# k^T v in four 64x64 tiles of the array instead of two of 96 rows, with a second bank and a sum

## The chip, the cores and the metric

The kernel runs on one core of a Trainium2 chip. The metric is the device time of one execution in microseconds (us); lower is better.

## The reference

An attention without softmax is followed by a SwiGLU feed-forward, all in fp32:

```python
q, k, v: (8, 8, 576, 64)          # batch, heads, sequence, head size
kv  = einsum('bhsd,bhse->bhde', k, v)       # k^T v: 64 x 64 for each head, summed over 576 rows
out = einsum('bhsd,bhde->bhse', q, kv)
out = out / sqrt(mean(out * out, -1) + 1e-6) * g_norm
x   = out.transpose(0, 2, 1, 3).reshape(4608, 512)
result = (silu(x @ w_gate) * (x @ w_val)) @ w_out      # 512 -> 1536 -> 512
```

The change touches only the first `einsum`: 8 batches x 8 heads, each a contraction over 576 rows into 64x64.

## The kernel before

The 4608 tokens are worked off in nine blocks of 512. `Att(n)` is the attention of block n. k^T v of one batch is needed for each of blocks 0 to 7. Block 0 is done at once, because nothing else can run before it; the attention of block n+1 is woven into the feed-forward of block n. The parts that the change and the argument touch:

```python
KP = 96
KT = S // KP                      # 576 = 96 x 6: six chunks of 96 rows
a_psum = pool("a_psum", 1, space=PS)        # one bank a buffer
b_psum = pool("b_psum", 2, space=PS)
c_psum = pool("c_psum", 2, space=PS)
m_psum = pool("m_psum", 3, space=PS)

# class Att
def load(self, room=None):
    self.load_q()
    # ...
    for j in range(NS):                             # 4 head pairs
        hs = slice(2 * j, 2 * j + 2)
        for i, (tiles, src) in enumerate(((self.k, k), (self.v, v))):
            if room:                                # block 0: a tile named h lends its room
                t = room.rearrange("p f t -> p (f t)")[:, (2 * j + i) * 2 * KT * D :]
            else:
                t = ld_pool.tile([P, 2 * BLK], F32, name="ld")
            t = t[0:KP, 0 : 2 * KT * D].rearrange("p (h x) -> p h x", h=2)
            nc.sync.dma_start(out=t, in_=src[self.n, hs].rearrange("h (p t) d -> p h (t d)", t=KT))
            tiles.append(t.rearrange("p h (t d) -> p h t d", t=KT))

def kv(self, js):
    # ...
    if js[0] == 0:
        self.kv_ps = m_psum.tile([P, NS, D], F32, name="m")
    for j in js:
        for c in range(KT):
            for u in range(2):                      # two heads: two column positions
                nc.tensor.matmul(
                    self.kv_ps[u * D : (u + 1) * D, j, :], lhsT=self.k[j][:, u, c, :],
                    rhs=self.v[j][:, u, c, :], start=(c == 0), stop=(c == KT - 1),
                )
    if js[-1] == NS - 1:
        nc.scalar.copy(out=kvs[self.n % 3], in_=self.kv_ps)

def turn_q(self, i):                                # q into [d, token], through m_psum
    # ...
def product(self, i, pools=None):                   # q . kv: 64x64 in four positions, two banks
    # ...
    for u in range(2):
        sq = sq_pool.tile([P, 2, NS, D], F32, name="sq")
        nc.scalar.activation(out=sq, in_=self.ps[i][u], func=ACT.Square)
        nc.vector.tensor_reduce(out=self.z[:, i, u], in_=sq, axis=mybir.AxisListType.X, op=OP.add)

# program order
blocks[0].load(room)              # q, k, v of block 0: DMA issues on SyncE
weights(1)                        # five weight loads, also on SyncE; one weight rounded on VectorE/ScalarE
scaled = blocks[0].all()          # turn_q, kv, product, root, scale, turn_x
# ... block 0: plain_up (12 x), then plain_down(0), kv and turn_q of block 1,
#     plain_down(1..3) with block 1's product and the rest between
# ... blocks 1 to 8: loads of the next block, up(), down(), with two kv calls of two head pairs each
```

All DMA loads are issued by SyncE, in program order. `weights` also gives work to VectorE (four operations for each weight piece, named g, u, u and wg in the trace) and to ScalarE. Each engine has one list of instructions, whose order a scheduler fixes when the program is built.

## Time and profile before

| before | value |
|---|---|
| time, median of 6 runs | 1116.32 us (1115.74 to 1117.8) |
| span of the profiled run | 1113.7 us |
| TensorE busy | 98% of the span |
| k^T v: instructions in blocks 1 to 7, and in block 0 | 672 and 96 |
| start to first feed-forward matmul | 33.58 us |
| a k^T v call of two head pairs, block 2 | 1.55 us |

A timeline has a row for each group: start us, length us, engine, line, operation, out<-in, count, and in brackets the idle time before it and what ended it; "SPq" rows are DMA issues on SyncE.

Block 1: k^T v, the turn of q and the output matmuls of block 0 (L559) share TensorE. From the timeline of TensorE before, 127 to 136 us:

```profile
127.17 1.62 PE L237 MATMUL m<-ld 96*64 96x64 f32 x48
128.72 1.09 PE L251 MATMUL m<-ident,ld 128*128 128x128 f32 x8
...
131.52 0.92 PE L237 MATMUL m<-ld 96*64 96x64 f32 x24 [0.53 <-DMA ld<-in_v_dram]
...
134.79 0.92 PE L237 MATMUL m<-ld 96*64 96x64 f32 x24
```

Two head pairs come in one piece, then one, then one, with the turn of q between them.

### The profile page before, as it was taken

The page shows a single profiled execution, that of the slowest core. Times are in us where ns is not written, and L with a number is a line of the kernel's source. Part 1 is how long each engine was busy: PE and PEld are TensorE (multiplying, and loading weights), DVE is VectorE, ACT ScalarE, POOL GpSimd, SP SyncE. Part 2 cuts the span into 40 slices and gives each one's busy share as a digit, 9 for nine tenths or more (in the row PEclk, how much of TensorE's full clock was granted, in tenths as well). Part 3 has the DMA queues.
Part 4 walks back from the last instruction along what each step waited for, and adds up shares of the span by engine and source line. Part 5 has one row for each costly group of instructions (what it writes and reads, how often), then busy time and mean ns, then how long its engine had stood idle before and what let it go on. Part 6 is the DMA issues. An engine that isn't in the chain of part 4 may idle for free.

```text
span 1113.7 us, 15512 instructions
## 1 busy us (share of the span) xinstructions
PE 1092.4 (98%) x6528; PEld 901.2 (81%) x6528; DVE 444.2 (40%) x759; ACT 272.4 (24%) x460; POOL 401.0 (36%) x320
## 2 busy tenths in 40 slices
PE   5999999999999999999999999999999999999998
PEld 4444548888888888888888888888888888888887
DVE  2999333126322551156113721263124621561221
ACT  2655112222122212222222122221222122222210
POOL 0021003452344334442444334532543345424550
PEclk9999999999999999999999999999999999999999
DMA  9677410310122010300040012101200100000001
GB/s 273 194 221 186 109 54 19 86 39 1 39 51 51 23 38 26 77 23 26 13 102 23 1 39 61 42 22 38 52 19 1 38 1 1 1 30 10 1 1 38
DMA packets 70245, 57.62 MB, mean 52 GB/s; under 512 B 39456, under 2 KB 64032, under 8 KB 70176
## 3 DMA queue, kind: packets, MB, share of 16 engines
q1 hardware_dynamic: 70112, 56.63, 18.9%
q8 instruction: 51, 0.84, 0.3%
q14 instruction: 18, 0.15, 0.0%
q0 software_dynamic: 64, 0.00, 0.0%
HBM read 47.19 MB, written 9.44 MB: 51 GB/s over the span
## 4 chain that ended last, share of the span: by engine, by line
PE 89%; DVE 1%; DMA 0%; issue 0%
PE b L383 45%; PE c L383 22%; PE a L383 11%; PE b L559 4%; PE m L237 2%; PE m L271 2%; PE m L315 1%; PE m L251 1%; PE b L546 0%; PE c L546 0%; DVE u L150 0%; DMA ld<-in_v_dram 0%; DVE wo L154 0%; DVE g L149 0%; PE a L271 0%; DVE u L144 0%
## 5 line engine op out<-in xcount | busy, mean ns | idle before, releaser
L110 POOL TENSOR_TENSOR t<-wg,wv 128x512 f32<-128x512 f32 x96 | 123.9, 1292 | 182.5 <-PE b L383 92.0
L110 POOL TENSOR_TENSOR t<-wv 128x512 f32<-128x512 f32 x48 | 63.9, 1331 | 323.9 <-PE c L383 117.8
L109 DVE TENSOR_TENSOR s<-h 128x256 f32<-128x256 f32 x48 | 20.4, 425 | 307.8 <-POOL h L111 307.8
L110 POOL TENSOR_TENSOR t<-wo 128x512 f32<-128x512 f32 x72 | 91.4, 1269 | 121.5 <-PE c L383 70.6
L383 PE MATMUL b<-x,t 128*128 128x256 f32 x384 | 91.3, 381 | 0.8
L383 PE MATMUL b<-x,wg 128*128 128x256 f32 x384 | 92.0, 382 | 0.0
L109 DVE TENSOR_TENSOR u<-c,u 128x512 f32<-128x512 f32 x96 | 65.9, 687 | 63.1 <-ACT u L425 63.1
L383 PE MATMUL a<-x,wg 128*128 128x256 f32 x384 | 90.9, 379 | 0.0
L383 PE MATMUL c<-xs,t 128*128 128x256 f32 x384 | 90.8, 379 | 0.0
L383 PE MATMUL b<-xs,t 128*128 128x256 f32 x384 | 90.8, 379 | 0.0
L383 PE MATMUL c<-xs,wv 128*128 128x256 f32 x384 | 90.7, 379 | 0.0
L383 PE MATMUL b<-x,wv 128*128 128x256 f32 x384 | 90.7, 379 | 0.0
L383 PE MATMUL b<-t,h 128*128 128x256 f32 x384 | 86.3, 381 | 0.0
L383 PE MATMUL b<-wo,h 128*128 128x256 f32 x384 | 85.8, 379 | 0.0
L398 ACT COPY u<-b 128x512 f32<-128x512 f32 x56 | 32.8, 586 | 214.2 <-PE b L383 214.2
L383 PEld LDWEIGHTS b<-x,t 128*128 128x128 f32 x384 | 72.3, 190 | 12.0 <-issue 2.5
L383 PEld LDWEIGHTS c<-xs,t 128*128 128x128 f32 x384 | 72.9, 190 | 10.3 <-issue 0.4
L383 PEld LDWEIGHTS b<-xs,t 128*128 128x128 f32 x384 | 72.9, 190 | 10.1 <-issue 0.3
L383 PEld LDWEIGHTS b<-x,wv 128*128 128x128 f32 x384 | 73.0, 190 | 9.9
L383 PEld LDWEIGHTS c<-xs,wv 128*128 128x128 f32 x384 | 73.0, 190 | 9.9
L383 PEld LDWEIGHTS a<-x,wg 128*128 128x128 f32 x384 | 73.0, 190 | 9.9
L111 POOL TENSOR_TENSOR h<-s,u 128x512 f32<-128x512 f32 x48 | 60.9, 1269 | 54.7 <-DVE u L109 54.7
(88 smaller groups left out, 1534.5 us busy)
## 6 DMA issues: line engine op xcount, KB each, us to landing
out_dram<-o SPq DMA_DIRECT2D x18, 512.0 KB, 2.8
ld<-in_q_dram SPq DMA_DIRECT2D x32, 256.0 KB, 5.0
ld<-in_k_dram SPq DMA_DIRECT2D x28, 288.0 KB, 4.6
ld<-in_v_dram SPq DMA_DIRECT2D x28, 288.0 KB, 4.1
ld<-in_moe_w_gate_dram SPq DMA_DIRECT2D x12, 512.0 KB, 4.8
ld<-in_moe_w_val_dram SPq DMA_DIRECT2D x12, 512.0 KB, 5.2
ld<-in_moe_w_out_dram SPq DMA_DIRECT2D x12, 512.0 KB, 4.1
h<-in_k_dram SPq DMA_DIRECT2D x4, 288.0 KB, 6.2
```

The source lines that it names most:

```text
L109: add = lambda e, o, a, b: e.tensor_tensor(out=o, in0=a, in1=b, op=OP.add)
L110: sub = lambda e, o, a, b: e.tensor_tensor(out=o, in0=a, in1=b, op=OP.subtract)
L111: mul = lambda e, o, a, b: e.tensor_tensor(out=o, in0=a, in1=b, op=OP.mult)
L237: nc.tensor.matmul(self.kv_ps[u * D : (u + 1) * D, j, :], lhsT=self.k[j][:, u, c, :], rhs=self.v[j][:, u, c, :], start=(c == 0), stop=(c = ...
L251: nc.tensor.transpose(ps[:, j], self.q[t][:, j], ident)
L271: nc.tensor.matmul(self.ps[i][u][p : p + D, t, j, :], lhsT=self.qt[rows, 2 * i + t, j, p : p + D], rhs=kvs[b % 3][rows, j, :], start=True, ...
L315: nc.tensor.transpose(ps[:, e, t], xt[:, t, j + e], ident)
L383: nc.tensor.matmul(self.ps[name][:, e], lhsT=lhsT, rhs=rhs, start=first and (e, i) == (0, 0), stop=i == self.steps - 1, skip_group_check=True,
L398: nc.scalar.copy(out=self.u2, in_=self.ps["b"])
L559: nc.tensor.matmul(ps, lhsT=self.h[:, f, P * t : P * (t + 1)], rhs=wo[:, f, :], start=(f == 0), stop=(f == NF - 1),)
```

## The change

The intent is to fill the array better in k^T v. A matmul of 96 rows and 64 columns leaves a quarter of the rows empty. With chunks of 64 rows, two chunks of the sequence can be in the array at once, the upper rows and the lower rows, each for two heads: four tiles. Rows of the upper and of the lower half add into different banks, and VectorE sums the two at the end. 576 rows are nine chunks of 64, so the upper half takes five and the lower four.

```diff
-    KP = 96
-    KT = S // KP
+    KT = 5
@@ load
-                    t = t[0:KP, 0 : 2 * KT * D].rearrange("p (h x) -> p h x", h=2)
-                    nc.sync.dma_start(out=t, in_=src[self.n, hs].rearrange("h (p t) d -> p h (t d)", t=KT))
+                    t = t[:, 0 : 2 * KT * D].rearrange("p (h x) -> p h x", h=2)
+
+                    for r, s0, m in ((0, 0, KT), (1, KT * D, KT - 1)):
+                        nc.sync.dma_start(
+                            out=t[r * D : (r + 1) * D, :, 0 : m * D],
+                            in_=src[self.n, hs, s0 : s0 + m * D].rearrange("h (p t) d -> p h (t d)", t=m),
+                        )
@@ kv
-                self.kv_ps = m_psum.tile([P, NS, D], F32, name="m")
+                self.kv_ps = [m_psum.tile([P, NS, D], F32, name="m") for _ in range(2)]
             for j in js:
                 for c in range(KT):
-                    for u in range(2):
-                        nc.tensor.matmul(
-                            self.kv_ps[u * D : (u + 1) * D, j, :], lhsT=self.k[j][:, u, c, :],
-                            rhs=self.v[j][:, u, c, :], start=(c == 0), stop=(c == KT - 1),
-                        )
+                    for r in range(2 if c < KT - 1 else 1):
+                        rows = slice(r * D, (r + 1) * D)
+                        for u in range(2):
+                            nc.tensor.matmul(
+                                self.kv_ps[r][u * D : (u + 1) * D, j, :], lhsT=self.k[j][rows, u, c, :],
+                                rhs=self.v[j][rows, u, c, :], start=(c == 0), stop=(c == KT - 1 - r),
+                            )
             if js[-1] == NS - 1:
-                nc.scalar.copy(out=kvs[self.n % 3], in_=self.kv_ps)
+                dst = kvs[self.n % 3]
+                nc.scalar.copy(out=dst, in_=self.kv_ps[0])
+                add(nc.vector, dst, self.kv_ps[1], dst)
```

(The assertion of the shapes changes with it.)

More of the change, by code (lines that the diff above doesn't have):

```diff
@@ L68 @@
     NP = NF // 2
-    KP = 96
-    KT = S // KP
+    KT = 5
     eps = 1e-6
     assert NT == B * S and NT == NB * BLK and NB == B + 1 and S - BLK == BLK // B
-    assert 2 * D == P and H == 2 * NS and KP * KT == S and NS == 4
+    assert 2 * D == P and H == 2 * NS and (2 * KT - 1) * D == S and NS == 4
     def pool(name, bufs, **kw):
```

## The prediction

> **What bounds the kernel now.** I read the page's busy times first, then its chain of work that ended last, then the waits of TensorE, then the groups of the k^T v line against those of its neighbour in shape, and last the timeline of one k^T v call and of one q·kv product.
>
> The page's busy times and chain (the chain's second line gives shares of the span by line):
>
> ```profile
> PE 1092.4 (98%) x6528; PEld 901.2 (81%) x6528; DVE 444.2 (40%) x759; ACT 272.4 (24%) x460; POOL 401.0 (36%) x320
> PE 89%; DVE 1%; DMA 0%; issue 0%
> PE b L383 45%; PE c L383 22%; PE a L383 11%; PE b L559 4%; PE m L237 2%; PE m L271 2%; PE m L315 1%; PE m L251 1%; PE b L546 0%; PE c L546 0%; DVE u L150 0%; DMA ld<-in_v_dram 0%; DVE wo L154 0%; DVE g L149 0%; PE a L271 0%; DVE u L144 0%
> ```
>
> TensorE is the bound from end to end: a microsecond of its stream is a microsecond of the time. But the changed line, L237, holds only 2% of the chain, some 25 us. So even halving it could not give more than about 1.3%.
>
> The groups of TensorE (busy us, mean ns of one | idle before) and its waits (us in total, times, longest):
>
> ```profile
> L271 PE MATMUL m<-kv,qt 64*64 64x64 f32 x832 | 24.1, 229 | 0.5 <-ACT kv L242 0.5
> L237 PE MATMUL m<-ld 96*64 96x64 f32 x672 | 22.9, 224 | 0.5 <-DMA ld<-in_v_dram 0.5
> L237 PE MATMUL m<-h 96*64 96x64 f32 x96 | 6.2, 317 | 2.9 <-DMA h<-in_v_dram 2.9
> ...
> PE m L237 <- DMA h<-in_v_dram: 2.9, 4, 1.1
> PE m L271 <- ACT kv L242: 0.5, 1, 0.5
> ```
>
> L237 has 768 instructions where the code asks for 8 blocks x 48 matmuls = 384: each fp32 matmul is two instructions. The 96 on tile h are block 0, where k and v come in by DMA and TensorE waits for them. The 672 on ld are blocks 1 to 7, where only 0.5 us was waited. L271 is useful because it already has the new form, 64x64 in four places of the array.
>
> The timeline of TensorE around one k^T v call of block 2, and around one product (start us, length us, group):
>
> ```profile
> 200.31 1.89 PE L383 MATMUL b<-xs,t 128*128 128x256 f32 x8
> 202.13 1.62 PE L237 MATMUL m<-ld 96*64 96x64 f32 x48
> 203.68 1.99 PE L383 MATMUL b<-x,wg 128*128 128x256 f32 x8
> 205.51 1.89 PE L383 MATMUL c<-xs,t 128*128 128x256 f32 x8
> ...
> 252.72 0.22 PE L271 MATMUL m<-kv,qt 64*64 64x64 f32 x1
> 252.73 0.22 PE L271 MATMUL a<-kv,qt 64*64 64x64 f32 x1
> 252.74 0.22 PE L271 MATMUL m<-kv,qt 64*64 64x64 f32 x1
> 252.74 0.22 PE L271 MATMUL a<-kv,qt 64*64 64x64 f32 x1
> 252.78 0.22 PE L271 MATMUL m<-kv,qt 64*64 64x64 f32 x1
> ...
> 253.71 5.45 PE L383 MATMUL c<-t,s 128*128 128x256 f32 x24
> ```
>
> Starts, not lengths, are what to read: lengths overlap. The product's instructions start in fours and the next four starts 0.06 us later. Its 64 instructions lasted from 252.62 (its first start, just above the lines shown) to 253.71, 1.09 us or 17 ns each. The k^T v call took 48 instructions from 202.13 to 203.68, 1.55 us or 32 ns each. So two 96-row tiles side by side take about as long per step as four 64-row tiles. As equations with a step s and a fixed part f: 16s + f = 1.09 and 24s + f = 1.55, so s = 0.0575 us and f = 0.17 us. The passage in and out is the same for both: about 0.09 us before the first start, and the following group is 0.10 us longer (203.68 to 205.51 is 1.83 us where eight such matmuls usually take 1.73).
>
> **What the Trainium skill says.** TensorEngine Tiling (Array Packing), Key Properties: tiles run independently, weight loads included, and a change of the tiling mode drains the engine. The trace agrees with both: fours within 0.02 us, and about 0.2 us around each call; before and after alike leave and re-enter the full array, so this part stays. The same page, Gotcha 1: different row tiles must not be in one PSUM bank at once. That is why the change takes a second bank and a sum; the product before does it so with banks m and a. TensorE: Matmul & The Clock Gate, Part 3, has tiles of a pack starting about 4 ns apart; this trace's 0.01 us steps are compatible. VectorE: DVE Perf Modes, the section on the TRN2 errata, gives an fp32 add of N columns as (N+151)/0.96 ns, 424 ns for the 256 here; this trace has 425 ns for adds of that size (line L109, s from h), so that is my cost for the new add.
>
> **The change part by part.**
>
> *Removed and added on TensorE.* Before, a head pair needs 6 chunks of 96 rows: 6 x 2 instructions = 12 steps of two places each. After, 576 rows are 9 chunks of 64; the upper rows take 5, the lower 4, at the same time. The longer side sets it: 5 x 2 = 10 steps, eight of four places and two of two. Instructions rise from 768 to 1152, but steps fall from 12 to 10. This is the point where the change is easily overrated: it does not go from two places to four at equal work, because 96 rows already filled three quarters of the array. A call of two head pairs goes from 24s + f = 1.55 to 20s + f = 1.32 us: 0.23 us saved. Blocks 1 to 7 have two calls' worth each: 14 x 0.23 = 3.2 us. All of this lies on the path, since TensorE has no idle there.
>
> *Block 0.* Each head pair there waits for its DMA, so only the last one's shortening counts. Its 24 instructions ran 1.55 us, less the last one's 0.31 is 1.24 for 12 steps, 0.10 a step; two fewer save 0.2 us.
>
> *The sum on VectorE.* One add a block, 0.43 us, 3.4 us of VectorE's time in all, after ScalarE's copy (0.37 us each). In blocks 1 to 7 the result is wanted by the product some 35 us later (216 to 253 in block 2), and VectorE is 40% busy: nothing on the path. In block 0 the product follows at once (its wait on the copy, 0.5 us, is above), so the add comes on top: with a semaphore about 0.5 us more.
>
> *PSUM.* k^T v takes two of the three m buffers instead of one. In blocks 2 to 7 both are copied out by about 219 and the next use of m is the turn of q at 241: no wait. In block 1, where k^T v and the turn of q are interleaved (127 to 136 us), the turn has one free buffer instead of two, but the scheduler has matmuls of L559 to put between. I allow 0.3 us for this with the loads below.
>
> *The loads.* Each k or v tile now comes in two DMAs, of 1280 and 1024 bytes a run where it was 1536; the bytes are the same. SyncE issues one in about 0.45 us, so eight more cost 3.6 us of issue in block 0, where the eight issues now end at 8.5 and the data land until about 16.6. The issue would end near 12.4, still ahead of the landings, which are limited by bandwidth (about 270 GB/s in that stretch, against about 348 GB/s later while 1024-byte runs of weights come). The shorter runs may even come faster. I take -0.3 us for it, in the range from -1 to +0.7. From block 2 on the loads have many microseconds in hand.
>
> Sum: -3.2 (blocks 1 to 7) -0.2 (block 0's last pair) +0.5 (block 0's add) -0.3 (block 0's loads) +0.3 (block 1's buffers and late loads) = -2.9 us. From 1116.95 this gives 1114.0 us.
>
> **The rivals.** (1) The row tiles do not run beside each other: then a call has 36 steps of two, +0.7 us a call, +10 us in all, about 1127. Against it: the product's fours, with one row tile in m and the other in a. Accumulation differs, as the product never accumulates; but k^T v accumulates now at the same 0.0575 a step. (2) The packing gives twice the rate on the whole of L237: 14 x 0.7 = 10 us, about 1107. Against it: the row count, 5 steps against 6. (3) The start turns the gain round: twice the DMA issues and VectorE's place in block 0 (it is busy with rounding weights, in order, and the add could come behind such work, each piece 0.4 to 0.7 us) delay the first product by 1 to 3 us; then about 1116 to 1117. For it: the start is the one place where TensorE waits. Against it: bandwidth, not issue, sets the landings. (4) A new static order of instructions around block 1 costs or gives 1 to 2 us; I see no way to know.
>
> **Range and chances.** The three runs before lie from 1115.8 to 1117.8, so ±1 us is noise. With ±1.5 us for the start and block 1 and ±1 for the step I get 1111.0 to 1117.0 for 8 in 10. A change of 2% would be 22 us, nearly all of L237's time; only rival 1 together with a broken schedule could approach it upwards. Faster 0.01, within 2% 0.98, slower 0.01.
>
> **What would show it right or wrong.** The k^T v groups should be 64x64 with 1008 and 144 instructions, 72 in a call; a call in block 2 should last 1.3 us from first start to the next matmul, with starts in fours. The groups' busy time should fall from 22.9 to about 20 us for blocks 1 to 7. In block 0 the wait before the product should move from ScalarE's copy to VectorE's add, about 0.9 to 1.0 us after the last k^T v. No new wait of TensorE on PSUM should show in blocks 2 to 8. I am wrong if the starts come in twos for a whole call, if the first product starts after 19.5 us, or if the matmuls of the turn of q in block 1 wait for copies for more than 1 us.

## More of the kernel before

From the timeline of the kernel before, 8 to 25 us:

```profile
8.01 0.45 SPq L215 DMA_DIRECT2D h<-in_v_dram  x1
8.98 0.39 SPq L133 DMA_DIRECT2D ld<-in_moe_w_gate_dram  x1
...
16.66 1.55 PE L237 MATMUL m<-h 96*64 96x64 f32 x24 [0.57 <-DMA h<-in_v_dram]
...
18.03 0.43 DVE L149 TENSOR_SCALAR g<-ld 128x512 uint32<-128x512 uint32 x1 [9.55 <-DMA ld<-in_moe_w_gate_dram]
18.67 1.99 PE L271 MATMUL m<-kv,qt 64*64 64x64 f32 x64 [0.46 <-ACT kv L242]
...
23.32 0.26 PE L271 MATMUL b<-kv,qt 64*64 64x64 f32 x1 [1.40 <-issue]
24.15 0.60 ACT L280 ACTIVATE sq<-b 128x512 f32<-128x512 f32 x1 [0.71 <-PE b L271]
24.78 1.28 DVE L281 TENSOR_REDUCE z<-sq 128x8 f32<-128x512 f32 x2 [1.94 <-ACT sq L280]
```

The eighth and last load of k or v is issued at 8.01 us and the first weight right behind it. The weight reaches VectorE at 18.03, the first product starts at 18.67, and the last reduction of its squares comes at 24.78, after a wait for ScalarE's squares. From there a chain of small operations leads to the first feed-forward matmul.

## The result, and the profile after

The changed kernel took 1114.71 us in the median of six runs (1114.33 to 1115.29), against 1116.32 us before. The ratio is 0.9984, with a 95% interval of 0.9971 to 0.9997: within 2%, and inside the predicted range. A ratio here is always the mean time of one kernel's runs over the mean of the other's of the same rounds, so it is not quite the ratio of the medians. Of the 2.9 us predicted, about 1.6 came in the medians and 1.3 in the profiled spans (1113.7 to 1112.4).

The groups of TensorE after the change (columns as in the prediction):

```profile
L245 PE MATMUL m<-ld 64*64 64x64 f32 x1008 | 20.5, 222 | 0.7 <-DMA ld<-in_v_dram 0.7
...
L245 PE MATMUL m<-h 64*64 64x64 f32 x144 | 7.1, 317 | 2.4 <-DMA h<-in_v_dram 2.4
```

k^T v of blocks 1 to 7 fell from 22.9 to 20.5 us busy with half as many instructions again. That of block 0 (on tile h) rose from 6.2 to 7.1. The timeline of TensorE after the change, around the k^T v call in block 2 that the prediction shows:

```profile
203.68 1.38 PE L245 MATMUL m<-ld 64*64 64x64 f32 x72
204.99 1.99 PE L393 MATMUL b<-x,wg 128*128 128x256 f32 x8
```

The call lasts from 203.68 to 204.99, 1.31 us, where 1.55 were used before and 1.32 were predicted. Inside it the instructions start in fours 0.058 us apart. (The row doesn't show this, since both banks are named m. It was counted in narrower windows.)

So the step of the array was right, and the rest of the saving was lost elsewhere. I divided each profiled span at three points: the first feed-forward matmul, block 1's first k^T v, and block 1's first product.

| us | start to first feed-forward matmul | to block 1's first k^T v | to block 1's first product | to the end |
|---|---|---|---|---|
| before | 33.58 | 93.58 | 16.39 | 970.12 |
| after | 34.28 | 93.55 | 17.27 | 967.29 |
| difference | +0.70 | -0.03 | +0.88 | -2.83 |

The last column holds the twelve calls of blocks 2 to 7: 12 x 0.23 = 2.8 us, as measured. The start lost 0.70 us, and block 1 lost 0.88 in spite of a saving of its own of 2 x 0.23. Over half of the gain was given back there. From the timeline after, at the start:

```profile
13.81 1.26 SPq L216 DMA_DIRECT2D h<-in_v_dram  x2
15.12 0.59 SPq L132 DMA_DIRECT2D ld<-in_moe_w_gate_dram  x1
...
16.98 1.83 PE L245 MATMUL m<-h 64*64 64x64 f32 x36 [0.48 <-DMA h<-in_v_dram]
18.35 0.37 ACT L251 COPY kv<-m 128x256 f32<-128x256 f32 x1 [8.45 <-PE m L245]
18.93 0.42 DVE L108 TENSOR_TENSOR kv<-m,kv 128x256 f32<-128x256 f32 x1 [10.37 <-PE m L245]
19.41 1.99 PE L281 MATMUL m<-kv,qt 64*64 64x64 f32 x64 [0.60 <-DVE kv L108]
20.18 0.68 ACT L140 ACTIVATE u<-ld 128x512 f32<-128x512 uint32 x1 [1.46 <-DMA ld<-in_moe_w_gate_dram]
20.18 0.43 DVE L148 TENSOR_SCALAR g<-ld 128x512 uint32<-128x512 uint32 x1 [0.83 <-DMA ld<-in_moe_w_gate_dram]
...
24.86 0.60 ACT L290 ACTIVATE sq<-b 128x512 f32<-128x512 f32 x1
25.33 0.61 ACT L290 ACTIVATE sq<-c 128x512 f32<-128x512 f32 x1
25.49 1.28 DVE L291 TENSOR_REDUCE z<-sq 128x8 f32<-128x512 f32 x2 [0.96 <-ACT sq L290]
```

Four things are to be seen. A load takes 0.60 to 0.61 us to issue where it took 0.45, so the sixteen end at 15.07 instead of 8.46, and the first weight is issued 6.1 us later. It reaches VectorE 2.15 us later (20.18 against 18.03). The new add itself ends at 19.35, before that weight is there. And the last reduction, which begins the chain to the first feed-forward matmul, waits 0.96 us for ScalarE. From 20.18 to 25.33 ScalarE does six operations on weights (u) and the four squares, one after the other. It is idle there for only 0.24 us, for the second weight, and never for the product. So in the changed kernel the late weight sets the start through ScalarE. From the timeline of TensorE after, in block 1:

```profile
127.83 1.38 PE L245 MATMUL m<-ld 64*64 64x64 f32 x72
129.14 0.66 PE L261 MATMUL m<-ident,ld 128*128 128x128 f32 x4
...
131.72 0.80 PE L245 MATMUL m<-ld 64*64 64x64 f32 x20 [0.70 <-DMA ld<-in_v_dram]
132.45 0.33 PE L261 MATMUL m<-ident,ld 128*128 128x128 f32 x1
132.71 0.68 PE L245 MATMUL m<-ld 64*64 64x64 f32 x16
...
135.77 1.08 PE L245 MATMUL m<-ld 64*64 64x64 f32 x36
```

The turn of q (L261), which now has one free m buffer, is in small pieces. The third head pair is cut in two by one of them (20 and 16 instructions), and the last one takes 1.02 us to the next matmul (135.77 to 136.79) where half a call should take about 0.75.

### The profile page after: what moved, and what is told of

Read it like the earlier page. It is cut to its first block, busy times and chain, and to the rows that moved or that the text cites. A ratio compares the mean times of both kernels' runs of the same rounds, so it can differ in the third digit from the quotient of the medians.

```text
span 1112.4 us, 16379 instructions
## 1 busy us (share of the span) xinstructions
PE 1090.7 (98%) x6912; PEld 899.1 (81%) x6912; DVE 447.5 (40%) x767; ACT 272.4 (24%) x460; POOL 400.9 (36%) x320
## 4 chain that ended last, share of the span: by engine, by line
PE 89%; DVE 1%; DMA 0%; issue 0%
PE b L393 45%; PE c L393 22%; PE a L393 11%; PE b L569 4%; PE m L281 2%; PE m L245 2%; PE m L325 1%; PE m L261 1%; PE b L556 0%; PE c L556 0%; DVE u L149 0%; DMA ld<-in_v_dram 0%; DVE wo L153 0%; DVE g L148 0%; PE a L281 0%; DVE u L143 0%
```

## The experiments

The theory after the result: the array's saving is real; the start loses because loads of 64 partitions hold up the weights on SyncE, not because of the add; block 1 loses because the second bank takes a buffer from the turn of q. The rivals: the add is to blame at the start, or twice the number of loads in itself, or the static order of instructions. In the runs below, "start" and the other parts are the four columns above. Each part comes from one profiled execution of each kernel, so tenths of a microsecond in the start can be chance: two profiles of the changed kernel gave 34.28 and 34.27 there, but 17.27 and 17.73 in block 1 (the second waited 0.44 us more for a v). In six profiles (e1, e3, e4, e6, e8 and e11) the granted clock of TensorE was 0.50 for 7 to 11 us between 25 and 37 us. Their second part is 93.57 to 93.87 us, against 93.40 to 93.64 in the others. Why the clock fell there stays open. The three groups (the first four runs, the next four, the last four) ran on three chips, each beside its own runs of the kernel before.

### e1_alternate: no odd step between two head pairs

The side with five chunks alternates with the head pair, so that the last odd chunk of one pair and the first of the next lie in different rows. Edit against the changed kernel:

```diff
-                    for r, s0, m in ((0, 0, KT), (1, KT * D, KT - 1)):
+                    ms = (KT, KT - 1) if j % 2 == 0 else (KT - 1, KT)
+                    for r, s0, m in ((0, 0, ms[0]), (1, ms[0] * D, ms[1])):
@@ kv
-                for c in range(KT):
-                    for r in range(2 if c < KT - 1 else 1):
+                o = j % 2
+                for c in range(KT) if o == 0 else (KT - 1, *range(KT - 1)):
+                    for r in range(2) if c < KT - 1 else (o,):
+                        # ... start and stop flags follow
```

> The changed kernel, with the five-chunk side alternating: upper rows take 5 chunks for even head pairs, lower rows for odd ones, so that the two odd chunks lie side by side. Theory (the longer side sets the steps, 0.058 us each): 18 steps a call instead of 20, the call in block 2 lasts 1.20 us instead of 1.31, and with 14 such calls the kernel is 1.6 us faster than the changed one, about 1113.1. Rival (the odd chunk's time is set by something else, such as instructions issued in order, 72 a call as before): the call stays at 1.3 us and the time at 1114.7.

Measured: 1114.51 us (1114.01 to 1115.32) against 1115.78 before, ratio 0.9991 [0.9978, 1.0003]. From its timeline of TensorE, block 2:

```profile
204.84 1.28 PE L249 MATMUL m<-ld 64*64 64x64 f32 x72
206.05 1.99 PE L397 MATMUL b<-x,wg 128*128 128x256 f32 x8
```

A call is 1.21 us with the same 72 instructions: 18 steps instead of 20, 0.05 us for each step saved. The last part of the span is 966.05, 1.24 us less than the changed kernel's, as 12 x 0.10 asks. So **steps, not instructions, are what a call costs**. The start (34.70) and block 1 (17.72) were 0.42 and 0.45 longer in this profile. The total missed what was expected (about 1113.1), and the result isn't told apart from the changed kernel's.

### e2_bank_a: block 1's second bank from another pool

```diff
-                self.kv_ps = [m_psum.tile([P, NS, D], F32, name="m") for _ in range(2)]
+                pools = (m_psum, a_psum if self.n == 1 else m_psum)
+                self.kv_ps = [pool.tile([P, NS, D], F32, name=pool.name[0]) for pool in pools]
```

> The changed kernel, but in block 1 alone the second bank comes from pool a, which is idle there, so that the turn of q has two m buffers again. Theory (block 1 lost its gain to the third m buffer): from the first k^T v of block 1 to its first product 16.2 to 16.5 us instead of 17.3, and 0.8 to 1 us faster, about 1113.9. Rival (the loads of v and k that are issued later cause it): at least 17 us still, and the time within 0.3 us of 1114.7.

Measured: 1114.35 us (1113.31 to 1115.01), ratio 0.9987 [0.9974, 0.9999]. Block 1's part fell from 17.27 to 16.56: 0.71 us came back. Of this, 0.17 is a shorter wait for v (0.53 instead of 0.70), which isn't the buffer's. Without the waits for v, block 1 took 15.86 us before, 16.57 after (16.61 in e8), 16.03 here and 16.14 in e7, which has the same bank. So the buffer cost some 0.5 us, the larger part of block 1's loss against the kernel before. The turn of q was whole again. Two lines of its TensorE timeline in block 1, the turn and the first instructions of the third head pair:

```profile
130.05 1.09 PE L262 MATMUL m<-ident,ld 128*128 128x128 f32 x8
...
132.54 0.59 PE L246 MATMUL m<-ld 64*64 64x64 f32 x13 [0.53 <-DMA ld<-in_v_dram]
```

What stays is 16.56 against 16.39 - 0.47 = 15.92 ideal. The second line shows part of it: thirteen instructions into bank m come first, before the first one into bank a. Two single head pairs took 1.00 and 0.96 us here. The built order lets one bank's matmuls run ahead, so four tiles aren't always in the array together. The start was longer in this profile (35.19), which took back the gain in the profiled run. The time missed the 1113.9 that was expected.

### e3_two_loads: the kernel before with each load in two of 48 partitions

```diff
-                    nc.sync.dma_start(out=t, in_=src[self.n, hs].rearrange("h (p t) d -> p h (t d)", t=KT))
+                    rows = src[self.n, hs].rearrange("h (p t) d -> p h (t d)", t=KT)
+                    for p0 in (0, KP // 2):
+                        nc.sync.dma_start(out=t[p0 : p0 + KP // 2], in_=rows[p0 : p0 + KP // 2])
```

> The kernel before, with each load of k and v cut in two of 48 partitions and nothing else changed. Theory (what counts is the issue of 16 instead of 8 loads a block, each of them costing SyncE about as much): the issue of block 0's loads ends near 12 to 15 us instead of 8.5, the first product starts 0.3 us later and block 1 loses up to 0.5 us; 0.3 to 0.8 us slower than before, about 1117. Rival (the loads' width of 64 partitions makes their issue dear): two of 48 cost no more than one of 96, and the time stays at 1116.3.

Measured: 1116.10 us (1115.62 to 1116.98), ratio 1.0005 [0.9993, 1.0018]. From its timeline of SyncE:

```profile
12.16 0.86 SPq L217 DMA_DIRECT2D h<-in_v_dram  x2
13.31 0.39 SPq L133 DMA_DIRECT2D ld<-in_moe_w_gate_dram  x1
```

A load of 48 partitions is issued in 0.43 us behind others (0.31 where nothing was under way), against 0.60 for one of 64. Sixteen of them end at 13.0 us. So neither the number alone (the theory) nor the width alone (the rival) explains the delay: of the first weight's 6.1 us later issue, 4.3 come with sixteen loads instead of eight (13.31 against 8.98) and 1.8 more with 64 partitions (15.12). At VectorE the weight came at 18.70, 0.67 later than before, and 1.48 earlier than in the changed kernel. The start was 0.52 longer than before. The first product came only at 20.23, since here ScalarE's list had two operations on the first weight ahead of its copy of kv. Block 1 was 0.55 shorter, because its wait of 0.53 for v was gone. So a loss in block 1 from later loads, which the theory expected, didn't come, and the total was the same.

### e4_rows_112: 112 partitions of five rows and 16 of one, in one bank

This goes from the kernel before, and asks whether row tiles were needed for the saving at all. Five chunks: the first of 128 rows, four of 112. No second bank, no sum, no row tiles.

```diff
-    KP = 96
-    KT = S // KP
+    KP = 112
+    KT = 5
@@ load
-                    nc.sync.dma_start(out=t, in_=src[self.n, hs].rearrange("h (p t) d -> p h (t d)", t=KT))
+                    nc.sync.dma_start(
+                        out=t[0:KP], in_=src[self.n, hs, 0 : KP * KT].rearrange("h (p t) d -> p h (t d)", t=KT)
+                    )
+                    nc.sync.dma_start(out=t[KP:P, :, 0:D], in_=src[self.n, hs, KP * KT : S].rearrange("h p d -> p h d"))
@@ kv
+                    rows = slice(0, KP if c else P)
                     for u in range(2):
                         nc.tensor.matmul(
-                            self.kv_ps[u * D : (u + 1) * D, j, :], lhsT=self.k[j][:, u, c, :],
-                            rhs=self.v[j][:, u, c, :], start=(c == 0), stop=(c == KT - 1),
+                            self.kv_ps[u * D : (u + 1) * D, j, :], lhsT=self.k[j][rows, u, c, :],
+                            rhs=self.v[j][rows, u, c, :], start=(c == 0), stop=(c == KT - 1),
                         )
```

> The kernel before with five chunks instead of six, without row tiles: 112 partitions hold five rows each and the last 16 partitions one row each, so that chunk 0 has 128 rows and the others 112. Ten steps a head pair as in the change, but one bank, no add, 640 instructions instead of 1152. Theory (the change's gain is steps, its losses are the add, the third buffer and the loads): the call in block 2 lasts 1.31 us, the first product does not wait for an add (0.6 us less than the changed kernel) and block 1 keeps its gain (0.9 us less), so about 1113.2. Rival (the gain needs four tiles at once, or 112 and 128 rows in turn cost a switch): the call stays at 1.5 us or more and the time at 1116 or above.

Measured: 1111.84 us (1110.90 to 1112.12) against 1115.78, ratio 0.9964 [0.995, 0.9977]. From its timeline of TensorE, block 2:

```profile
201.31 1.39 PE L241 MATMUL m<-ld 128*64 128x64 f32 x40
202.63 1.99 PE L387 MATMUL b<-x,wg 128*128 128x256 f32 x8
```

40 instructions in two tiles take 1.32 us, the same as 72 in four tiles. Both are 20 steps. So the whole gain of the change in the steady stage comes from ten steps a head pair instead of twelve, and none from four tiles as such. Here it is kept: the last part is 967.34, block 1's 15.51, and the start 33.36. Of the 0.88 that block 1 gained on the kernel before, 0.47 are steps and 0.53 the wait for v, which was gone as in e3 (other work took 0.12 more). The loads are sixteen as well, but of 112 partitions (0.42 us backlogged, 0.31 later) and of 16 (0.46), so the first weight is issued at 13.22 and is at VectorE at 17.91. That is 4.2 us later in issue than before, but 0.12 earlier in arrival. A later issue alone therefore needn't be a delay, though with almost the same issue (13.31) e3's weight arrived 0.67 later than before.

### e5_act_queue: block 0's lower halves issued by ScalarE

```diff
-                        nc.sync.dma_start(
+                        (nc.scalar if room is not None and r else nc.sync).dma_start(
```

> The changed kernel, with the lower halves of block 0's k and v loads issued by ScalarE's queue, so that SyncE issues 8 loads at 0.6 us before the first weights, not 16. Theory (block 0 loses its time because the weights' loads are issued at 15 us instead of 9, and VectorE's rounding of the first weight stands in order before the reduction of the first product): the first w_gate arrives near 18 us instead of 20.2, the first plain matmul starts at 33.0 to 33.7 instead of 34.3, and the kernel is 0.5 to 1.2 us faster than the changed one. Rival (block 0 loses it to the add, which stays): the first plain matmul stays at 34.1 or later and the time too.

Measured: 1117.54 us (1116.86 to 1118.18) against 1115.25, ratio 1.002 [1.0006, 1.0033]. It failed as a test. The trace shows SyncE waiting 3.8 us for one of these loads to land, and TensorE 8.9 us for q in four waits (4.8 in three in the changed kernel). The reason that I take from the built program, and that no trace shows, is that transfers take their semaphores from a rotation of eight, and ScalarE's loads took those that q and the rest needed. The first weight was issued at 15.31, no earlier than in the changed kernel, so nothing was learned about what an earlier weight is worth.

### e6_add_twice: the cost of one more VectorE operation in block 0

```diff
                 add(nc.vector, dst, self.kv_ps[1], dst)
+                if self.n == 0:
+                    nc.vector.tensor_tensor(out=dst, in0=dst, in1=dst, op=OP.max)
```

> The changed kernel, with a second VectorE operation of the same size (maximum of kv with itself, 0.43 us) after block 0's add, before the product. Theory (the weights' arrival sets the start, the add is beside it): the first product starts 0.45 us later, near 19.9, but the reduction of it still follows the rounding of the first weight, and the first plain matmul and the time stay within 0.2 us of the changed kernel's. Rival (the add is on the path, as predicted): first plain matmul and time 0.45 us later.

Measured: 1115.41 us (1113.77 to 1115.96), ratio 0.9999 [0.9986, 1.0011], beside 1114.85 for the changed kernel. From its timeline:

```profile
20.51 1.98 PE L283 MATMUL m<-kv,qt 64*64 64x64 f32 x64 [1.14 <-DVE kv L254]
20.68 0.43 DVE L148 TENSOR_SCALAR g<-ld 128x512 uint32<-128x512 uint32 x1 [0.32 <-DMA ld<-in_moe_w_gate_dram]
```

The first product came 1.10 us later than in the changed kernel (20.51 against 19.41), yet the first feed-forward matmul came only 0.52 later, just as the first weight did (20.68 against 20.18). In five profiles the start follows the weight and not the product:

| us | first weight at VectorE | first product | first feed-forward matmul | from weight to feed-forward |
|---|---|---|---|---|
| after | 20.18 | 19.41 | 34.28 | 14.10 |
| e8 (after again) | 20.14 | 19.44 | 34.27 | 14.13 |
| e1 | 20.57 | 19.29 | 34.70 | 14.13 |
| e2 | 21.13 | 19.27 | 35.19 | 14.06 |
| e6 | 20.68 | 20.51 | 34.80 | 14.12 |

In all five, ScalarE went from the first weight to the last square as in the lines of the changed kernel above: idle for 0.20 to 0.28 us, for the second weight, and never for the product, while VectorE waited 0.79 to 0.99 for it. So the theory was right that the weight decides, but named the wrong engine: it is ScalarE's list, and not the four operations on VectorE. **The add is off the path in block 0**, and the rival that blamed it falls.

### e7_all_three: e1, e2 and e5 together

The edit is the three diffs above in one kernel.

> The changed kernel with three mends: alternating five-chunk side (18 steps a call), block 1's second bank from pool a, block 0's lower halves issued by ScalarE's queue. If the losses found are separate: 1.4 us for the calls, 0.7 for block 1, 0.7 for the start, together 2.8 us less than the changed kernel, about 1111.9, level with five chunks of 112 rows (1111.8 in the call before). Rival (what one mend gives, another place takes): at most 1.5 us less.

Measured: 1116.57 us (1115.62 to 1117.08), ratio 1.001 [0.9997, 1.0022]. Calls were again 1.21 us and the last part 966.07, but the start was 38.47, by the waits of e5, and block 1 took 17.18, of which 1.04 are waits for v. The array's part adds up as expected; the total says nothing beyond what e5 said.

### e8_after_again: the changed kernel once more

No edit.

> The changed kernel itself, unaltered, so that the three above have it on the same chip. Expected: 0.998 to 0.999 of the kernel before; first w_gate at VectorE between 20 and 21.2 us, and the first plain matmul 14 us after it, as in the three profiles with this start so far.

Measured: 1114.85 us (1113.98 to 1117.09) against 1115.25 on this chip, ratio 0.9998 [0.9986, 1.0011]. So the gain of the change was 0.16% in the first session and 0.02% here, where the interval includes none: a gain in the total is barely shown. The last part was again 967.29 and the start 34.27; block 1 was 17.73.

### e9_halves_together: both halves of rows in one load

The order of the sequence rows over partitions is free, since k^T v sums over all of them. So a load of 128 partitions with four rows each feeds both halves, and a second one of 64 partitions brings the odd chunk. This should cure the pieces of block 1. Edit against the changed kernel:

```diff
-                    for r, s0, m in ((0, 0, KT), (1, KT * D, KT - 1)):
-                        nc.sync.dma_start(
-                            out=t[r * D : (r + 1) * D, :, 0 : m * D],
-                            in_=src[self.n, hs, s0 : s0 + m * D].rearrange("h (p t) d -> p h (t d)", t=m),
-                        )
+                    m = KT - 1
+                    nc.sync.dma_start(
+                        out=t[:, :, 0 : m * D], in_=src[self.n, hs, 0 : m * P].rearrange("h (p t) d -> p h (t d)", t=m)
+                    )
+                    nc.sync.dma_start(
+                        out=t[0:D, :, m * D :], in_=src[self.n, hs, m * P :].rearrange("h p d -> p h d")
+                    )
```

> The changed kernel with its loads cut otherwise: one load of all 128 partitions, four rows each, and one of 64 partitions, one row each, so that both row tiles have their data at once. Theory (a load of 64 partitions takes SyncE 0.60 us to issue, one of 96 or more 0.3 to 0.45; the start follows the arrival of the first weight, which waits for those issues; and a lower half that lands later keeps the row tiles from overlapping): first weights issued near 13 us instead of 15, first w_gate at VectorE near 18.5 to 19.3 instead of 20.1, the first plain matmul 14.1 us after it, a head pair in block 1 in 0.75 us instead of 1.0; 0.8 to 1.5 us faster than the changed kernel, so 0.9975 to 0.998 of before. Rival (add, bank and 64-row matmuls cost it, whatever the loads): within 0.3 us of the changed kernel.

Measured: 1119.48 us (1116.25 to 1120.17) against 1115.98, ratio 1.0023 [1.0011, 1.0036]. Slower, where I expected faster. The six runs fall in two groups, four from 1119.43 to 1120.17 and two at 1116.25 and 1116.98; the profile is of the slower group. From its timeline of TensorE in block 1:

```profile
133.34 0.80 PE L247 MATMUL m<-ld 64*64 64x64 f32 x36 [0.62 <-DMA ld<-in_v_dram]
...
138.69 1.33 PE L247 MATMUL m<-ld 64*64 64x64 f32 x36 [3.07 <-DMA ld<-in_v_dram]
```

The first line is what was wanted: a whole head pair in one piece, 0.73 us to the next matmul. The second line undoes it: 3.07 us of waiting for the last v. After this wait the granted clock was 0.50 to 0.65 until 142 us, so that this head pair took 1.27 us. At the start the issues were still 0.60 us each, those of 128 partitions too (later, with nothing under way, these took 0.37 and those of 64 again 0.60). So the width of a load isn't all that its issue depends on. The first weight was issued at 14.81, and there was a new stall of 2.2 us within the first product that the trace puts down to "issue" (TensorE waited for nothing that the profile shows).

### e10_together_alternate_a: e9 with e1 and e2

The edit is e9's loads, with e1's alternation and e2's bank.

> The kernel of e9 with the odd chunk in alternating rows (18 steps a call) and block 1's second bank from pool a. If the parts add up: 1.4 us for the calls and 0.5 for block 1 below e9, some 0.996 of before, level with five chunks of 112 rows or a little better. Rival: the start or block 1 takes it back, 0.998 or more.

Measured: 1119.02 us (1116.93 to 1119.98), ratio 1.0024 [1.0012, 1.0036]. The last part was 966.04, the best with e1's, but the start 36.34 and block 1 21.91. A miss for e9's reasons: 2.7 us of waits for v in block 1, a granted clock of 0.50 to 0.59 there from 138 to 145 us, and a stall of 2.36 on "issue" in the first product.

### e11_rows_112_again: e4 on another chip

No edit against e4.

> The kernel of e4 (five chunks of 112 and 128 rows, no row tiles) again, beside e9 and e10 on the same chip: 0.9955 to 0.997 of before, its calls 1.31 us, the first plain matmul near 33.4 us.

Measured: 1111.93 us (1111.50 to 1112.69) against 1115.98, ratio 0.9963 [0.995, 0.9976]. A call was 1.31 us, the start 33.84, later than expected. The gain of e4 holds on a second chip.

### e12_one_tail_load: e9 with block 0's eight small loads as two

```diff
             for j in range(NS):
+                if room and j == 1:
+                    for dst, src in zip(self.tail, (k, v)):
+                        nc.sync.dma_start(out=dst[0:D], in_=src[self.n, :, (KT - 1) * P :].rearrange("h p d -> p h d"))
@@ load, for each tile
-                    nc.sync.dma_start(
-                        out=t[0:D, :, m * D :], in_=src[self.n, hs, m * P :].rearrange("h p d -> p h d")
-                    )
+                    if not room:
+                        # ... the same load
```

> The kernel of e9, with block 0's eight small loads replaced by two that bring all heads' last rows, so that block 0 needs 10 loads and not 16. Theory (the weights' issue sets the start): weights issued near 9.5 us as in the kernel before, first w_gate near 18, the first plain matmul 0.5 to 1 us earlier than in e9, with the add still there. VectorE's order now has the first weight's operation ahead of the add, so the product starts near 19. Rival (the add sets the start): no gain over e9.

Measured: 1115.11 us (1114.45 to 1116.63), ratio 0.9993 [0.9981, 1.0005]. From its timeline:

```profile
17.49 0.43 DVE L148 TENSOR_SCALAR g<-ld 128x512 uint32<-128x512 uint32 x1 [8.93 <-DMA ld<-in_moe_w_gate_dram]
...
22.72 0.37 PE L293 MATMUL m<-kv,qt 64*64 64x64 f32 x2 [2.40 <-issue]
```

Ten loads of block 0 instead of sixteen let the weight go at 10.65 and arrive at 17.49, earlier than in the kernel before. It was 4 us faster than e9 in the median. But of the 4.5 between the two profiles only 1.44 lie in the start; 3.08 lie in block 1, where the loads are the same as in e9, but the waits for v were 1.67 instead of 3.69 and the clock stayed at 1.00. So most of it isn't the weight's. The start was 34.73, no better than the changed kernel's: in the last line the first product stands still for 2.40 us on "issue". So a late weight is not the only thing that can set the start. Such a stall was also there in the kernel before, 1.40 us in its product into b and c, in e4 and e11 (1.5 each), e9 (2.2), e10 (2.4), e7 (1.25), e3 (0.60) and e5 (0.35). It was not in the product of the changed kernel, e1, e2, e6 or e8.

What goes with it is the fetch of instructions. The DMA view lists transfers of the instruction queue. Each of the nine profiles with the stall has one packet of 16 KB ahead of it: before at 20.7 us, e4 at 21.0, e9 at 21.7, e12 at 20.1, and so on. In all nine, TensorE goes on 2.2 to 2.7 us after the packet. In the changed kernel the packet comes at 16.6, while TensorE waits for v anyway, and 2.7 us later the product hasn't begun. The same is true of e1, e2, e6 and e8. From the DMA view of the changed kernel, window 16 to 18 us:

```profile
q8 instruction: 1, 0.02, 3.5%
```

In e6 it came at 17.4, and there it was the last k^T v of block 0 that took 2.59 us instead of 1.83. I take it that more k^T v instructions ahead of the product moved the point where a fetch is due, to a harmless place in the changed kernel. This is a coincidence in time, though a regular one, in all fourteen profiles. No run isolates it.

## Why the prediction was right

The time and the range held, and so did the largest term. That the time held is in part luck: the range, 1111.0 to 1117.0, also holds the 1116.32 of the kernel before, and the terms for the start and for block 1 were wrong without being large enough to leave it. Of the sum, the steps one by one:

- **Removed and added on TensorE**: predicted 1.32 us a call, measured 1.31; predicted 0.23 saved a call, and twelve calls gave 2.83 us. The two equations of the prediction, with s = 0.0575 us for a step, held for four tiles that accumulate. e1 (18 steps, 1.21) and e4 (20 steps of two tiles, 1.32) show that steps are the right count. Rivals 1 and 2 fall: starts came in fours, and the rate did not double. "TensorE is the bound from end to end" holds for these blocks but not for the start of 34 us, where another engine sets the pace.
- **Block 0's k^T v**, predicted -0.2: it went the other way. The upper half's loads land first, and the built order takes its chunks before the lower ones; the last pair took 1.83 us instead of 1.55. The step "two fewer steps save 0.2" assumed that both halves are there together. The sign was wrong, but it cost nothing, as the weight came later still.
- **The sum on VectorE**, predicted +0.5 in block 0. Its own duration was right, 0.42 us (the 424 ns that the prediction works out from the formula of the Trainium skill is an estimate). But it took the place of ScalarE's copy on the path instead of coming on top: with the upper half early, the copy ran under the lower half's matmuls (18.35), and the wait ahead of the product rose only from 0.46 to 0.60. The sign that was named, an add 0.9 to 1.0 us after the last k^T v, didn't come. The product itself was off the path (e6). So the predicted +0.5 is about 0.1 before the product and nothing in the time.
- **The loads**, predicted -0.3: this is the step that failed at the start. "SyncE issues one in about 0.45 us" was wrong for 64 partitions, which took 0.60 to 0.61. The step "still ahead of the landings, which are limited by bandwidth" asked only when k and v land, and not what stands in the queue behind them: the first weight, 6.1 us later in issue and 2.15 in arrival. It cost +0.70 us in the start, all loads and their consequences together. Rival 3 named the doubled issues, but had them and the add delay the first product on VectorE. The product came 0.74 later and was off the path; the path led through ScalarE. How the weights' delay of 2.15 became 0.70 can be read there. ScalarE took up the first weight 1.67 later than before (20.18 against 18.51; before, it had to copy kv first, and so began 0.48 after the weight's arrival). In the kernel before it then idled for 1.10 before the last square, 0.39 for the product and 0.71 for the stalled product into b and c; in the changed one it idled for 0.24. With 0.13 from the operations themselves, the last square starts 0.68 later. So the stall of the kernel before hides 0.71 us; without it the start would have lost about 1.4 (an estimate from these waits).
- **Block 1**, predicted +0.3 for buffers and late loads, measured 0.88 + 0.47 = 1.35. Some 0.5 of it is the buffer (e2). "The scheduler has matmuls of L559 to put between" was true: TensorE didn't wait for a bank in block 1, so the sign of more than 1 us of such waits never showed. The cost came as small pieces instead. From start to start, the same sixteen turns of q took 2.32 us instead of 2.01 before and 1.86 in e2, and k^T v took 3.67 instead of 3.24 and 3.27. Another 0.5 is the two single head pairs at 1.00 and 0.96 us in e2, where e9 and e4 have 0.73. Of the rest, 0.17 is a longer wait for v, which differs from profile to profile.

The sum as measured in the profiles is -2.83 + 0.70 + 0.88 - 0.03 = -1.3 us, against -2.9 predicted. Both are within 2% of the time. That the first product would stay before 19.5 us as a sign of health was fulfilled (19.41) and was the wrong sign. As predicted, TensorE didn't wait for a bank in blocks 2 to 8. Open are: why a load of 64 partitions takes longer to issue than one of 48 or 112, and makes others between it slow as well; what causes the "issue" stall; and why the first weight arrives between 20.1 and 21.1 us in kernels with the same loads of block 0.

## What to carry to other kernels

Count steps of the array (the longest side of what runs together), not tiles or instructions: nine chunks on two sides are ten steps (five, of two instructions each), and so are five chunks of 112 and 128 rows in one bank, which gave the same 1.32 us without a second bank, a sum or more instructions, and a total 0.36% below the kernel before. Before you split a load, look at what is queued behind it on the issuing engine and at every engine that works on what it brings (here the slower list was ScalarE's, not VectorE's), and measure the issue time of the new shape. A buffer taken from a pool is paid for where another user of the pool is interleaved, here in block 1 alone and not in the steady stage, and it can cost time without any wait for it in the trace.

## What the Trainium skill lacked or had wrong

- DMA: Bandwidth & Descriptors, section "Issuing engines are not separate DMA queues", says of the time to initiate a DMA that it is "usually small relative to the DMA itself". A load of blocks 1 to 7 landed 2.9 to 3.3 us (medians) after its issue in the changed kernel, so 0.60 is the smaller part; but issues add up on one engine, and sixteen of 0.60 to 0.61 us moved the first weight's issue from 8.98 to 15.12 us. The issue time by shape would have been needed there. The runs show, for loads of two runs a partition, 0.60 us with 64 partitions (also with nothing else under way), 0.31 unloaded and 0.43 to 0.45 backlogged with 48 or 96, 0.31 to 0.42 with 112, and with 128 partitions 0.37 unloaded and 0.60 between loads of 64.
- Runtime: NRT & Kernel Launch, section "Instruction fetch mechanics", calls the cost of crossing a 16 KiB boundary "mostly hidden". In nine of fourteen profiles a stall of TensorE of 0.35 to 2.4 us ends 2.2 to 2.7 us after a 16 KB packet of the instruction queue at the start, where the DMA engines of the kernel before are 90% busy or more. The link is a coincidence in time and not shown by an experiment, but it is worth a warning for the first microseconds of a kernel.
